# GpSimd's long subtractions in four pieces, v's halves made by ScalarE and VectorE, and v's largest turned one slot after its last product

## The chip, the core and the metric

The kernel runs on one core of a Trainium2 chip. The metric is the device time of one execution in microseconds, as the median of several executions. TensorE multiplies matrices, VectorE, ScalarE and GpSimd work on vectors, and SyncE issues DMAs. Each engine runs its own row of instructions in order; between engines there are only semaphores.

## What is computed

Three layers follow one another on the same activations, 4 batches of 576 positions:

```python
# 1: causal attention with decay, 8 heads of 64
scores = q @ k.T / 8 + cum[:, None] - cum[None, :]      # cum = cumsum(log f)
x = softmax(causal(scores)) @ v                         # heads side by side: 512 columns
# 2: low-rank mixing over positions, then a feed-forward part
u = x + (x.T @ U @ V).T                                 # U 576x32, V 32x576
y = u + relu(u @ w_ch1) @ w_ch2                         # 512 -> 2048 -> 512
# 3: four experts, each a causal attention of its own, the best two per position
q, k, v = y @ wq[e], y @ wk[e], y @ wv[e]
out += gate[e] * (softmax(causal(q @ k.T / 8)) @ v @ wo[e])
```

The result has float32 accuracy although the products run on narrower inputs: nearly every operand is held as two halves, a rounded one (name ending in `h`) and the rest that rounding left (ending in `l`), and a product is the sum of three matmuls, high by high, high by low and low by high.

## The kernel before

**Stages.** The first attention takes heads in pairs `p` = 0 to 15, four pairs a batch. For pair `p` the scores are multiplied and made into exponentials while the row maxima of pair `p+1` are found and the inputs of pair `p+2` loaded. The pairs of batch 0 run alone (the loop over `range(NP)`); in the pairs 4 to 15 (`later_batches`) matmuls of the feed-forward part of earlier batches are woven in by `fill`. Then the rest of the feed-forward part runs by itself (`fill_until`), and at the end the second attention with 16 heads `h`, four experts `e` for each batch `b`.

**What sets the order.** In `later_batches` and in the second attention the order on TensorE is the order of the code (`manual_schedule`). Everywhere else, and for all other engines throughout, a scheduler orders the instructions by times that it estimates while the program is built; an instruction that is made longer, shorter or moved to another engine can therefore change the order of others.

**The high and low halves.** `ffn_load` (L344) reads a block of 288 positions as `ust` [128, 4, 288], ScalarE rounds it to `uh` (L351), and GpSimd makes `ul` in one subtraction of 1152 columns (L352). In `ffn_hidden` (L359) eight matmuls take `uh`, and then four, one for each of the four slices of 288 columns, take `ul`. `load_y` does the same for the second attention with `yh` and `yl` (L770, L771). The weights' halves `w1l` and `w2l` (L341) are GpSimd subtractions too, of 512 columns, behind three VectorE operations on `wst` (L303, L305, L306).

**The values.** `value_scale` (L244) finds the largest |v|: VectorE reduces each partition to `am` (L247), TensorE turns that column into a row `amt` (L250), VectorE reduces the row to one number `ar`, whose exponent alone is kept (L252 to L254), TensorE spreads it over the partitions (`rsp`, L259), and VectorE's reciprocal gives `rs` (L261). `value_parts` (L264) multiplies `vr` by `rs` and 8192 on VectorE (L266), rounds it to float16 on ScalarE, `vh` (L267), and subtracts on GpSimd, `vl` (L268). `weighted_values` (L226) multiplies them with the two halves of the exponentials, `ph` and `pl` (L219, L220).

**The second attention's slots.** For each head the loop issues the first half of the scores (five matmuls), a slot, the second half (twelve), a slot, the products `ua` and `ub` for the row maxima of head `h+2` (L154, L162), a slot, the weighted values `av` of the head before, two slots, and the transposition `mt` of the row maxima (L178). A slot, `work_on(n)`, takes the next `n` pieces of the generators in `work`: projections `pq` of the next batch (`experts_qk`), its values `pv` and gates (`expert_values`), and the output products of the batch before (`expert_out`). A generator's `yield` ends a piece. The `ub` products need the score buffers (`ps2`, two of them), which ScalarE's exponentials `pf` (L218) empty.

Of the kernel before, what the change touches and what calls it, by code (L numbers as in the profile page):

```python
# [13 lines left out]
AF = mybir.ActivationFunctionType  # L14
OP = mybir.AluOpType
# [3 lines left out]
B, H, S, D = 4, 8, 576, 64  # L19
# [5 lines left out]
NT = 5  # L25
# [26 lines left out]
def f32(ap):  # L52
    return ap.bitcast(F32)
# [3 lines left out]
def kernel(  # L57
# [49 lines left out]


    ones1 = const.tile([1, P], BF16, name="ones1")
    nc.gpsimd.memset(ones1[:], 1.0)  # L110

    def make_heads(pl_, n, decay):

# [149 lines left out]

    def value_parts(vr, rs, vh, vl):  # L264

        nc.vector.tensor_scalar(vr, vr, rs[:, 0:1], VEXP, OP.mult, OP.mult)  # L266
        nc.scalar.copy(vh[:, :, :, 0:64], vr)  # L267
        nc.gpsimd.tensor_tensor(vl[:], vr, vh[:, :, :, 0:64], OP.subtract)  # L268

    def row_scales(av, rs, extra=None):  # L270

        den = small.tile([P, NT], F32, name="den")
        nc.vector.tensor_scalar(den[:], av[:, :, 64:65].rearrange("p t o -> p (t o)"),
                                1.0e-9 * PSCALE * VEXP, rs[:, 0:1], OP.add, OP.mult)
        rn = small.tile([P, NT], F32, name="rn")
        nc.vector.reciprocal(rn[:], den[:])
        if extra is not None:
            nc.vector.tensor_tensor(rn[:], rn[:], extra, OP.mult)
        return rn
# [64 lines left out]
    def ffn_load(b, c, first, fy):  # L344
        fu = cur["fu"]
        cs = slice(c * HC, c * HC + HC)
        ust = fy.tile([P, KT, HC], F32, name="ust", tag="yc")
        nc.sync.dma_start(ust[:], udram[b, :, :, cs])
        uh = fu.tile([P, KT, HC], F32R, name="uh")
        ul = fu.tile([P, KT, HC], F32R, name="ul")  # L350
        nc.scalar.copy(uh[:], ust[:])  # L351
        nc.gpsimd.tensor_tensor(ul[:], ust[:], f32(uh[:]), OP.subtract)  # L352
        if first:
            return uh, ul, ust
        yc = fy.tile([P, KT, HC], F32, name="yc", tag="yc")
        nc.sync.dma_start(yc[:], ydram[b, :, :, cs])
        return uh, ul, yc
# [109 lines left out]
    for i in range(2):  # L467
        vh_ = hpool.tile([P, 2, NT, 65], F16, name=f"vh{i}")
        vl_ = hpool.tile([P, 2, NT, 64], F16, name=f"vl{i}")
        nc.gpsimd.memset(vh_[:, :, :, 64:65], VEXP)  # L470
        vhs.append((vh_, vl_))
    NPAIR = B * NP
    st_in, st_rs, st_p = {}, {}, {}
# [287 lines left out]
    def load_y(b, yp, stp, tag):  # L761
        yh = yp.tile([P, KT, SP_], F32R, name="yh", tag="yh")
        yl = yp.tile([P, KT, SP_], F32R, name="yl")
        nc.gpsimd.memset(f32(yh[:, :, S:SP_]), 0.0)
        nc.gpsimd.memset(f32(yl[:, :, S:SP_]), 0.0)
        for c in range(NC):
            cs = slice(c * HC, c * HC + HC)
            st = stp.tile([P, KT, HC], F32, name="yst", tag=tag)
            nc.sync.dma_start(st[:], ydram[b, :, :, cs])
            nc.scalar.copy(yh[:, :, cs], st[:])  # L770
            nc.gpsimd.tensor_tensor(yl[:, :, cs], st[:], f32(yh[:, :, cs]), OP.subtract)  # L771
        return yh, yl

    y = load_y(0, sy0, fy, "yc")
# [80 lines left out]
    def expert_values(b, y):  # L855
# [4 lines left out]
        for t in range(NT):  # L860
# [6 lines left out]
                                     start=n == 0, stop=n == 3 * KT - 1)  # L867
                    n += 1
            nc.scalar.copy(vr[:, t, :], pv[:, 0:NV])
            yield  # L870
        vh = sy.tile([P, NT, E, 65], F16, name="vh3")
        vl = sy.tile([P, NT, E, 64], F16, name="vl3")
        nc.gpsimd.memset(vh[:, :, :, 64:65], VEXP)
        vv_ = vr[:, :, 0:E * D].rearrange("p t (e d) -> p t e d", e=E)
        rs = yield from value_scale(vv_)
        value_parts(vv_, rs, vh, vl)
# [90 lines left out]
    with tc.manual_schedule(engines={mybir.EngineType.PE}):  # L967
# [14 lines left out]
        for h in range(NH):  # L982
# [27 lines left out]
            work_on(2)  # L1010
            if m:
                one(m)
            if e == 3:
                work_on(2 if more else 1)
        expert_attend(B - 1, E - 1)
        work_on(100)
    for p_ in (ys[1], sy, att, hpool2, hpool, sy0, sw, small, psf, ps1, ps2, dram, const):
# [58 lines left out]
```

## Time and profile before

| | |
|---|---|
| median of 3 runs | 964.29 us (964.15 to 964.66) |
| profiled execution | 960.93 us |
| its span, first to last instruction | 959.2 us |
| mean granted TensorE clock | 0.944 |
| TensorE busy | 862.3 us (90%) |
| VectorE busy | 554.7 us (58%) |
| ScalarE busy | 416.5 us (43%) |
| GpSimd busy | 286.7 us (30%) |

In the rows below an engine's instruction stands with its line in the kernel, the tile that it writes and those that it reads. PE is TensorE, PEld its weight loads, DVE is VectorE, ACT is ScalarE and POOL is GpSimd. PEclk is the clock that TensorE was granted, 1.00 being full. A time in square brackets is how long the engine had nothing to do just before an instruction, followed by what ended that wait. An engine that is idle costs nothing unless TensorE, the busiest one, waits for it in the end.

### The profile page before, as it was taken

Reading aid. Unit: us, or ns where it says so; the run is one execution under the profiler, and the core shown is the slowest. Engines: PE = TensorE matmul, PEld = TensorE weight load, DVE = VectorE, ACT = ScalarE, POOL = GpSimd, SP = SyncE. Lnnn points to the kernel's source line nnn. Section 1 sums busy time; section 2 is a strip of 40 time slices with the busy share of each in tenths; the row PEclk is TensorE's granted clock in tenths of the full one; section 3 lists DMA queues with packets and bytes.
Section 4 is the critical chain, followed back from the end, with each engine's and each line's share of the span. In section 5 each row is a group of like instructions: output and inputs, shape, how many; then the busy total and the mean of one; then the engine's idle time right before and its main releaser. Section 6 shows DMA issues by size and latency. Waiting matters only on the chain.

```text
span 959.2 us, 19001 instructions
## 1 busy us (share of the span) xinstructions
PE 862.3 (90%) x7480; PEld 804.7 (84%) x7480; DVE 554.7 (58%) x1468; ACT 416.5 (43%) x784; POOL 286.7 (30%) x238
## 2 busy tenths in 40 slices
PE   4887778989999989989999999999999787999987
PEld 3766567888888878989999999999998787888965
DVE  7787677877666555542255652222225566667674
ACT  4556455655445544442134442222113444545454
POOL 8445354443433224021135333323023303001010
PEclk9987568999999999999999999999999787999999
DMA  6434454444533332103168653424006210212201
GB/s 172 136 84 133 146 155 140 120 133 130 138 108 84 104 109 60 52 14 112 50 222 286 217 203 111 149 73 127 28 26 183 65 40 12 75 38 65 49 36 66
DMA packets 68777, 101.94 MB, mean 106 GB/s; under 512 B 6608, under 2 KB 49424, under 8 KB 68688
## 3 DMA queue, kind: packets, MB, share of 16 engines
q1 hardware_dynamic: 64416, 92.47, 32.7%
q10 hardware_dynamic: 4272, 8.26, 2.3%
q8 instruction: 59, 0.97, 0.4%
q14 instruction: 30, 0.25, 0.1%
HBM read 60.33 MB, written 22.56 MB: 86 GB/s over the span
## 4 chain that ended last, share of the span: by engine, by line
PE 67%; DVE 12%; DMA 8%; ACT 6%; issue 4%; POOL 2%; SPq 1%; ACTq 0%; POOLq 0%; DVEq 0%
PE hps L366 19%; PE cps L381 18%; PE sc L209 8%; PE pq L823 4%; PE pv L866 3%; DMA ust<-udram 2%; DVE pl L220 2%; PE po L901 2%; PE av L236 2%; PE gp L548 2%; PE ub L162 2%; ACT pf L218 2%; DVE junk L173 2%; PE av L240 2%; PE av L238 2%
## 5 line engine op out<-in xcount | busy, mean ns | idle before, releaser
L381 PE MATMUL cps<-hh,w2h 128*128 128x288 f32 x512 | 156.3, 306 | 5.6 <-DVE yc L383 3.7
L381 PE MATMUL cps<-hh,w2l 128*128 128x288 f32 x512 | 153.1, 299 | 1.3 <-POOL w2l L341 1.3
L381 PE MATMUL cps<-hl,w2h 128*128 128x288 f32 x512 | 152.2, 297 | 0.0
L220 DVE TENSOR_TENSOR pl<-pf,ph 128x576 f16<-128x576 f32 x144 | 117.7, 823 | 51.8 <-ACT ph L219 51.2
L366 PE MATMUL hps<-uh,w1h 128*128 128x288 f32 x512 | 145.3, 305 | 0.2 <-ACT uh L351 0.2
L366 PE MATMUL hps<-uh,w1l 128*128 128x288 f32 x512 | 141.8, 299 | 0.0
L371 DVE SCALAR_TENSOR_TENSOR hl<-hps,hh 128x288 fp32r<-128x288 f32 x128 | 58.0, 453 | 119.1 <-ACT hh L370 119.0
L370 ACT ACTIVATE hh<-hps 128x288 fp32r<-128x288 f32 x128 | 52.3, 409 | 155.1 <-PE hps L366 154.9
L218 ACT ACTIVATE pf<-sc 128x576 f32<-128x576 f32 x144 | 84.0, 612 | 61.3 <-PE sc L209 55.9
L381 PEld LDWEIGHTS cps<-hh,w2h 128*128 128x128 f32 x512 | 97.9, 191 | 6.5 <-DVE yc L383 4.4
L381 PEld LDWEIGHTS cps<-hh,w2l 128*128 128x128 f32 x512 | 97.9, 191 | 1.5 <-POOL w2l L341 1.5
L366 PEld LDWEIGHTS hps<-uh,w1h 128*128 128x128 f32 x512 | 97.9, 191 | 0.6 <-ACT uh L351 0.4
L366 PEld LDWEIGHTS hps<-uh,w1l 128*128 128x128 f32 x512 | 97.9, 191 | 0.0
L381 PEld LDWEIGHTS cps<-hl,w2h 128*128 128x128 f32 x512 | 97.7, 191 | 0.0
L236 PE MATMUL av<-vh,ph 128*128 128x65 f16 x720 | 91.9, 206 | 1.9 <-DVE x L282 1.6
L366 PE MATMUL hps<-ul,w1h 128*128 128x288 f32 x512 | 89.4, 297 | 4.6 <-POOL ul L352 4.6
L238 PE MATMUL av<-vl,ph 128*128 128x64 f16 x720 | 90.5, 202 | 0.0
L240 PE MATMUL av<-vh,pl 128*128 128x65 f16 x720 | 90.0, 202 | 0.1
L209 PE MATMUL sc<-qa,ka 67*128 67x288 f32 (+4 forms) x288 | 83.0, 348 | 7.9 <-ACT pf L218 3.8
L219 ACT CAST ph<-pf 128x576 f16<-128x576 f32 x144 | 88.3, 638 | 1.6
L236 PEld LDWEIGHTS <-ph 128*128 128x128 f16 x720 | 70.9, 104 | 13.7 <-issue 5.6
L173 DVE CUSTOM_DVE_ANT_0 junk<-ub,maskm 128x448 bf16<-128x448 f32 x192 | 79.6, 414 | 3.2 <-PE ub L162 1.2
(160 smaller groups left out, 1966.1 us busy)
## 6 DMA issues: line engine op xcount, KB each, us to landing
raw<-in_w_dram SPq DMA_DIRECT2D x32, 512.0 KB
ust<-udram SPq DMA_DIRECT2D x22, 576.0 KB
qkt<-in_qk_dram SPq DMA_DIRECT2D x16, 576.0 KB
yc<-ydram SPq DMA_DIRECT2D x14, 576.0 KB
ydram<-yc SPq DMA_DIRECT2D x14, 576.0 KB
vr<-in_v_dram SPq DMA_DIRECT2D x16, 320.0 KB
udram<-ustage ACTq DMA_DIRECT2D x16, 288.0 KB
ydram<-ust SPq DMA_DIRECT2D x8, 576.0 KB
```

The costliest lines, as they stand in the source:

```text
L173: nc.vector.tensor_tensor_reduce(junk[0:n, 0:w], ub[0:n, bk, off:off + w], maskm[0:n, m0:m0 + w], 1.0, NEG, OP.add, OP.max, mx[0:n, t:t + 1])
L209: nc.tensor.matmul(ps[:, bk, off:off + w], wa, xa, start=bk not in banks[:n], stop=bk not in banks[n + 1:])
L218: nc.scalar.activation(pfv, view, AF.Exp, scale=ISC)
L219: nc.scalar.copy(ph[:, o0:o0 + n], pf[:, 0:n])
L220: nc.vector.tensor_tensor(pl[:, o0:o0 + n], pf[:, 0:n], ph[:, o0:o0 + n], OP.subtract)
L236: nc.tensor.matmul(av[0:m, it, :], ph[0:k, c:c + m], vh[0:k, jt, :], start=first, stop=False)
L238: nc.tensor.matmul(av[0:m, it, 0:64], ph[0:k, c:c + m], vl[0:k, jt, :], start=False, stop=False)
L240: nc.tensor.matmul(av[0:m, it, :], pl[0:k, c:c + m], vh[0:k, jt, :], start=False, stop=last)
L366: nc.tensor.matmul(ph[:], wa[:, k, fs], xa[:, k, :], start=n == 0, stop=n == 3 * KT - 1)
L370: nc.scalar.activation(hh[:], ph[:], AF.Relu)
L371: nc.vector.scalar_tensor_tensor(hl[:], ph[:], 0.0, f32(hh[:]), OP.max, OP.subtract)
L381: nc.tensor.matmul(pc[:], wa[:, t, dsl], xa[:], start=n == 0, stop=n == 3 * FT - 1)
```

## The change

The subtractions `ul` and `yl` are each issued as four, one for each slice of 288 columns. The scaling of `vr` is no longer an operation of its own: ScalarE scales while it rounds (`vh`), and VectorE scales and subtracts in one operation (`vl`). The factor 8192 moves into `ones1`, and so into `rs`; the column of `vh` that sums the exponentials holds 1 instead of 8192. In the second attention the last `pv` product and the reduction `am` are one piece, and the two extra slots after the fourth expert of a batch become one extra slot after each of the first two.

```diff
-    nc.gpsimd.memset(ones1[:], 1.0)
+    nc.gpsimd.memset(ones1[:], 1.0 / VEXP)
...
-        nc.vector.tensor_scalar(vr, vr, rs[:, 0:1], VEXP, OP.mult, OP.mult)
-        nc.scalar.copy(vh[:, :, :, 0:64], vr)
-        nc.gpsimd.tensor_tensor(vl[:], vr, vh[:, :, :, 0:64], OP.subtract)
+        nc.scalar.activation(vh[:, :, :, 0:64], vr, AF.Copy, scale=rs[:, 0:1])
+        nc.vector.scalar_tensor_tensor(vl[:], vr, rs[:, 0:1], vh[:, :, :, 0:64], OP.mult,
+                                       OP.subtract)
...
-                                1.0e-9 * PSCALE * VEXP, rs[:, 0:1], OP.add, OP.mult)
+                                1.0e-9 * PSCALE, rs[:, 0:1], OP.add, OP.mult)
...
-        nc.gpsimd.tensor_tensor(ul[:], ust[:], f32(uh[:]), OP.subtract)
+        for k in range(KT):
+            nc.gpsimd.tensor_tensor(ul[:, k], ust[:, k], f32(uh[:, k]), OP.subtract)
...
-            nc.gpsimd.tensor_tensor(yl[:, :, cs], st[:], f32(yh[:, :, cs]), OP.subtract)
+            for k in range(KT):
+                nc.gpsimd.tensor_tensor(yl[:, k, cs], st[:, k], f32(yh[:, k, cs]), OP.subtract)
...
             nc.scalar.copy(vr[:, t, :], pv[:, 0:NV])
-            yield
+            if t < NT - 1:
+                yield
...
-            if e == 3:
-                work_on(2 if more else 1)
+            if b == B - 1:
+                work_on(e == 3)
+            elif e < 2:
+                work_on(1)
```

The two `memset` lines of the `vh` column write 1.0 for `VEXP`. In the changed kernel the lines stand one to three further down from L352 on.

GpSimd's row in the feed-forward stage, before (`ul` of the blocks to come, `w1l` and `w2l` of the next quarter of the weights):

```order
L352 TENSOR_TENSOR ul<-ust,uh 128x1152 x3
L341 TENSOR_TENSOR w1l<-wst,w1h 128x4x128 x2
L352 TENSOR_TENSOR ul<-ust,uh 128x1152
L341 TENSOR_TENSOR w1l<-wst,w1h 128x4x128 x2
L352 TENSOR_TENSOR ul<-ust,uh 128x1152
L341 TENSOR_TENSOR w2l<-wst,w2h 128x512
L352 TENSOR_TENSOR ul<-ust,uh 128x1152
```

The same place in GpSimd's row of the changed kernel:

```order
L353 TENSOR_TENSOR ul<-ust,uh 128x288 x12
L341 TENSOR_TENSOR w1l<-wst,w1h 128x4x128 x2
L353 TENSOR_TENSOR ul<-ust,uh 128x288 x4
L341 TENSOR_TENSOR w1l<-wst,w1h 128x4x128 x2
L353 TENSOR_TENSOR ul<-ust,uh 128x288 x4
L341 TENSOR_TENSOR w2l<-wst,w2h 128x512
L353 TENSOR_TENSOR ul<-ust,uh 128x288 x4
```

Each long subtraction has become four; they keep their places among the weights' subtractions.

TensorE's row in the second attention, where batch 1's values end and the first head of batch 1 begins, before (`pv` values, `sc` scores, `amt` and `rsp` the two turns for v's largest):

```order
L866 MATMUL pv<-wah,yl 128x260
L178 MATMUL mt<-ident,mx_96 5x128
L250 MATMUL amt<-ident,am 1x128
L209 MATMUL sc<-qa_9049,ka_9051 128x288
...
L209 MATMUL sc<-maskt,identb 128x128
L259 LDWEIGHTS ones_87
L259 MATMUL rsp<-ar,ones_87 128x1
L209 MATMUL sc<-qa_9049,ka_9051 128x320
```

The same place in TensorE's row of the changed kernel:

```order
L868 MATMUL pv<-wah,yl 128x260
L178 MATMUL mt<-ident,mx_96 5x128
L209 MATMUL sc<-qa_9105,ka_9107 128x288
...
L209 MATMUL sc<-maskt,identb 128x128
L250 MATMUL amt<-ident,am 1x128
L209 MATMUL sc<-qa_9105,ka_9107 128x320
...
L259 LDWEIGHTS ones_87
L259 MATMUL rsp<-ar,ones_87 128x1
L154 MATMUL ua<-ka_8074,qa_8072 128x288 x2
```

`amt` has moved behind the first half of the scores, `rsp` behind the second half, and `ua` follows at once.

VectorE's row in the second attention, batch 3, before (`junk,mx` a piece of the row maxima, `gsm` and `gex` the gates):

```order
L261 RECIPROCAL rs<-rsp 128x1
L173 ISA junk,mx_98<-ub,maskm 128x192
L173 ISA mx_98 128x1
L806 TENSOR_REDUCE gsm<-gex 128x5
L266 TENSOR_SCALAR vr_11365<-vr_11365,rs 128x5x256
L173 ISA junk,mx_98<-ub,maskm 64x64
```

The same place in VectorE's row of the changed kernel:

```order
L261 RECIPROCAL rs<-rsp 128x1
L165 ISA junk,mx_98<-ua,maskm 128x576
...
L173 ISA junk,mx_98<-ub,maskm 128x448
L173 ISA mx_98 128x1
L809 TENSOR_SCALAR gsm<-gsm 128x5
L267 SCALAR_TENSOR_TENSOR vl_11560<-vr_11401,rs,vh_11559 128x1280
L173 ISA junk,mx_98<-ub,maskm 128x320
L173 ISA mx_98 128x1
```

Where the scaling stood before the last piece of the row maxima, `vl` now stands before the last three.

## Rows read from the trace of the kernel before

**Rows 1.** Stages: us; PE, PEld, DVE, ACT, POOL busy (instructions); PEclk, DMA share, GB/s.

```profile
0.00:128.00 128.00, 92.30 (x746) 79.01 (x747) 96.52 (x259) 70.72 (x125) 65.47 (x76) 0.83 0.47 139
128.00:430.00 302.00, 276.75 (x2680) 254.29 (x2680) 195.83 (x538) 151.79 (x281) 104.85 (x75) 0.95 0.35 101
430.00:722.00 292.00, 287.59 (x2164) 286.22 (x2161) 110.12 (x225) 79.00 (x148) 88.07 (x69) 0.99 0.41 132
722.00:959.20 237.20, 205.64 (x1901) 185.15 (x1899) 152.27 (x446) 114.98 (x230) 28.27 (x21) 0.93 0.24 64
```

**Rows 2.** TensorE's timeline: start us, duration us, instruction, idle before it.

```profile
138.29 1.01 PE L162 MATMUL ub<-ka,qa 66*128 66x448 f32 x2 [3.55 <-ACT pf L218]
...
249.29 0.79 PE L366 MATMUL hps<-ul,w1h 128*128 128x288 f32 x4 [1.86 <-POOL ul L352]
...
513.62 0.61 PE L381 MATMUL cps<-hh,w2h 128*128 128x288 f32 x1 [2.10 <-DVE yc L383]
...
538.97 0.40 PE L381 MATMUL cps<-hh,w2h 128*128 128x288 f32 x1 [1.25 <-DVE yc L383]
...
803.97 0.37 PE L250 MATMUL amt<-ident,am 128*1 128x128 f32 x1 [3.86 <-DVE am L247]
...
807.44 0.16 PE L259 MATMUL rsp<-ar,ones 1*128 1x1 bf16 x1 [1.93 <-DVE ar L254]
```

**Rows 3.** Short stretches behind four of these stalls, columns as in the first group.

```profile
139.00:144.00 5.00, 5.00 (x46) 4.85 (x45) 3.13 (x11) 1.20 (x4) 0.09 (x1) 0.50 0.57 185
...
514.00:517.00 3.00, 3.00 (x14) 3.00 (x14) 1.08 (x4) 0.93 (x2) 1.28 (x1) 0.50 0.55 183
539.00:542.00 3.00, 3.00 (x23) 3.00 (x23) 1.77 (x5) 0.62 (x1) 1.29 (x1) 1.00 0.62 200
...
804.00:813.00 9.00, 7.07 (x31) 6.66 (x32) 7.15 (x19) 4.80 (x8) 4.90 (x2) 0.50 0.01 3
```

**Rows 4.** VectorE's timeline, operations with two inputs in SBUF.

```profile
133.29 3.19 DVE L220 TENSOR_TENSOR pl<-pf,ph 128x576 f16<-128x576 f32 x1
...
247.79 2.06 DVE L220 TENSOR_TENSOR pl<-pf,ph 128x576 f16<-128x576 f32 x1 [1.59 <-ACT ph L219]
...
501.34 0.69 DVE L305 SCALAR_TENSOR_TENSOR wst<-raw,wst 128x512 int32<-128x512 int32 x1 [0.42 <-ACT raw L304]
...
510.73 2.46 DVE L305 SCALAR_TENSOR_TENSOR wst<-raw,wst 128x512 int32<-128x512 int32 x1 [0.80 <-ACT raw L304]
...
535.85 2.70 DVE L305 SCALAR_TENSOR_TENSOR wst<-raw,wst 128x512 int32<-128x512 int32 x1 [1.53 <-ACT raw L304]
...
803.84 2.61 DVE L791 TENSOR_TENSOR gt<-vr 128x80 f32<-128x80 f32 x1
```

**Rows 5.** GpSimd's timeline at 249 and 510 us.

```profile
249.20 1.88 POOL L268 TENSOR_TENSOR vl<-vr,vh 128x640 f16<-128x640 f32 x1
...
509.99 2.65 POOL L352 TENSOR_TENSOR ul<-ust,uh 128x1152 fp32r<-128x1152 f32 x1 [0.52 <-PE cps L381]
```

**Rows 6.** Groups by line and shape, GpSimd: count, busy us, mean ns, idle before.

```profile
L748 POOL TENSOR_TENSOR wal<-st,wah 128x512 fp32r<-128x512 f32 x4 | 5.2, 1293 | 22.1 <-ACT wah L747 22.1
...
L748 POOL TENSOR_TENSOR wal<-st,wah 128x260 fp32r<-128x260 f32 x4 | 3.0, 749 | 11.9 <-ACT wah L747 11.9
```

**Rows 7.** The same view, the scaling and the rounding of v.

```profile
L266 DVE TENSOR_SCALAR vr<-vr,rs 128x640 f32<-128x640 f32 x16 | 14.4, 898 | 0.1
...
L266 DVE TENSOR_SCALAR vr<-vr,rs 128x1280 f32<-128x1280 f32 x4 | 4.0, 1008 | 0.1
...
L267 ACT CAST vh<-vr 128x640 f16<-128x640 f32 x16 | 11.7, 729 | 11.2 <-DVE vr L266 11.2
...
L267 ACT CAST vh<-vr 128x1280 f16<-128x1280 f32 x4 | 5.1, 1264 | 7.6 <-DVE vr L266 7.6
```

**Rows 8.** The chain that ended last, at 807 us: start us, us, what.

```profile
807.60 2.67 PE sc L209 x12
```

**Rows 9.** The page's group of ScalarE's exponentials.

```profile
L218 ACT ACTIVATE pf<-sc 128x576 f32<-128x576 f32 x144 | 84.0, 612 | 61.3 <-PE sc L209 55.9
```

More of the change, by code (lines that the diff above doesn't have):

```diff
@@ L469 @@
         vl_ = hpool.tile([P, 2, NT, 64], F16, name=f"vl{i}")
-        nc.gpsimd.memset(vh_[:, :, :, 64:65], VEXP)
+        nc.gpsimd.memset(vh_[:, :, :, 64:65], 1.0)
         vhs.append((vh_, vl_))
@@ L869, in expert_values @@
             nc.scalar.copy(vr[:, t, :], pv[:, 0:NV])
-            yield
+            if t < NT - 1:
+                yield
         vh = sy.tile([P, NT, E, 65], F16, name="vh3")
         vl = sy.tile([P, NT, E, 64], F16, name="vl3")
-        nc.gpsimd.memset(vh[:, :, :, 64:65], VEXP)
+        nc.gpsimd.memset(vh[:, :, :, 64:65], 1.0)
         vv_ = vr[:, :, 0:E * D].rearrange("p t (e d) -> p t e d", e=E)
```

## Prediction

> **What bounds the kernel now.** I read the page first, then the engines' busy time by stage, then TensorE's stalls in order of time, then the granted clock behind each stall, and last what VectorE and GpSimd did there. By stage [rows 1] this is four programs, with TensorE the busiest engine in all but the first: to 128 us the first attention alone (TensorE busy 92.3 of 128 us), to 430 us attention and feed-forward woven together (276.8 of 302), to 722 us feed-forward alone (287.6 of 292), then the second attention (205.6 of 237.2). The time to be had is TensorE's idle time, 36, 25, 4 and 32 us, and what follows it.
>
> What follows is the clock. TensorE's stalls of 3.55 us at 138 us and 2.10 us at 514 us [rows 2] stand ahead of stretches at 0.50, the lower of the two levels (1.2 against 2.4 GHz); behind the stall of 1.25 us at 539 us it stays at 1.00 [rows 3]. In the second attention 804 to 813 us is at 0.50, behind a stall of 3.86 us.
>
> Several of these stalls begin on VectorE while GpSimd works. A rearranging operation on `wst` takes 0.69 us when GpSimd is quiet, and 2.46 and 2.70 us beside a long `ul` subtraction. `pl` takes 3.19 us, where its 576 columns at the quiet rate make 0.78; `gt`, 80 columns, takes 2.61 us beside `yl` [rows 4]. The held one ends an ordinary duration after GpSimd's instruction does: `ul` from 509.99 ends at 512.64 [rows 5], the `wst` operation at 513.19. So a long GpSimd subtraction holds VectorE's two-input operations until its own end.
>
> The Trainium skill, page "SBUF — State Buffer", section "Who interferes with whom", says that a VectorE instruction with two SBUF inputs and a GpSimd instruction that reads SBUF exclude each other, the first to issue keeping the shared ports for its whole length. The holds above agree. The rule also speaks against this change, as the second rival below.
>
> **Part 1: `ul` and `yl` in four pieces.** On GpSimd 512 columns take 1.293 us and 260 take 0.749 [rows 6]; on the line through both, a piece of 288 takes 0.81 us. Four take 3.24 us where one takes 2.65, so a hold shrinks to at most 0.81 us, and the last quarter comes 0.6 us later.
>
> At 133 us: `pl` starts at 133.29 and ends at 136.48; held by one piece at most, it ends by 133.29 + 0.81 + 0.78 = 134.9. The `ub` stall of 3.55 us hangs on it through the `pf` buffer and ScalarE: −1.6 us. Between 0 (another wait there ends as late) and −1.6 − 2.5, the half of the 5 us at 0.50 from 139 us [rows 3].
>
> At 510 us: the first piece of `ul` ends at 510.80, so `wst` at 511.5 instead of 513.19, and the addition to `yc` behind it follows; the stall of 2.10 us becomes 0.4, below the 1.25 us that left the clock alone. −1.7, and −1.5 for half of the 3 us at 0.50: −3.2 us (between −1.0, if part of the hold stays, and −3.6).
>
> At 536 us: `wst` ends by 535.85 + 0.81 + 0.69 = 537.35 instead of 538.55: −1.2 us (0 to −1.25, the whole stall).
>
> Twice, at 249 us and in the same way at 359 us, TensorE waits for `ul` itself, 1.86 us [rows 2]. Each `ul` matmul now waits for its own piece, but the four stand together behind the `uh` ones and the last needs the last piece: 0.6 us later, less three of four matmuls already done (the four take 0.79 us). That is +0.2 at each. If VectorE's `pl` of 0.78 us gets a turn between two pieces, another 0.8 at one of them: +1.2 us together, between −1 and +2. The other loads come early enough that another step's hidden matmuls cover 0.6 us.
>
> **Part 2: v's halves.** Out go 20 scalings on VectorE (16 at a mean of 0.898 us, 4 at 1.008, holds included [rows 7]) and 20 subtractions on GpSimd. In come 20 VectorE subtractions with two SBUF inputs, at the quiet rate of `wst` 0.86 us for 640 columns and 1.7 for 1280; ScalarE's 20 conversions stay (0.729 and 1.264 us), now started by `rs` instead of by the scaling. VectorE's time stays the same sixteen times and grows by 0.7 us four times. If the new ones are held as well, by 0.81 us each, it is 16 us more. In the woven stage, where TensorE is 92% busy, matmuls cover them: 0; with that cover gone 12 times 0.81, 10 us. GpSimd's freed time counts for nothing by itself. The new part is a wait: `vl` stands in VectorE's row and waits for ScalarE's `vh`; queued behind it are row maxima and the division by the sums, which TensorE waits for. That is the third rival. The `memset` constants cost nothing: the same instructions with another value.
>
> **Part 3: the turns.** The largest of v (`am`) is now issued with the last v product, and its transposition `amt` comes behind the next head's first five score matmuls; the twelve others then stand ahead of `rsp`. Twelve took 2.67 us [rows 8], so five take 1.1. Batch 1, from 800 us: `amt` waits 3.86 us because ScalarE's last copy of v stands behind two `yh` copies, which the new order leaves there. The five go into that stall, and the twelve into the 1.93 us before `rsp` [rows 2]. But the `pq` products that stood between the scores and `ub` are gone from there, so `ub` waits for two exponentials of 0.612 us [rows 9]: −1.1 − 1.9 + 1.2 = −1.8. Batch 0, from 749 us: twelve scores that ran before `amt` run after it, while `am` ends at the same time: +2.7, of which I take four fifths to fall into the waits that now stand behind `amt` (`rsp`, then `ub`): +0.5. Batch 3, from 910 us: `vl` (1.7 us, after a `vh` of 1.26) stands before three of the row maxima that `mt` waits for; of these 2.9 us I take two thirds to lie beside the `av` products: +1.0. Batch 2 keeps its pattern: 0. Sum −0.3 us, between −4 (the stalls go, and the clock stretch behind one shortens) and +4 (nothing saved in batch 1, the two losses larger).
>
> **The first attention** is ordered by the scheduler on TensorE too, and the new operations have reshuffled it on every engine. I find no chain that is clearly longer or shorter: 0, between −3.6 and +3.6, a tenth of its 36 idle microseconds [rows 1].
>
> **Sum.** −1.6 − 3.2 − 1.2 + 1.2 − 0.3 = −5.1 us. The profiled execution took 960.93 us (span 959.2), so 955.8 after. The median of the runs shown is 964.29, 3.36 us above that execution: I predict 959.2 us.
>
> **Rivals.** 1. *The clock gives more back.* If the stalls at 138 and 804 us get short enough, 5 us at 0.50 behind the one and 9 us (TensorE busy for 7.07 of them [rows 3]) behind the other run at full rate: 2.5 + 3.5 us more, 953.2 us. For: the 1.25 us stall left the clock up. Against: by my own sums about 2 and 2.8 us of these two stalls remain.
>
> 2. *Taking turns.* Behind one long hold VectorE was free; now each of `gt`, `eq` and `pl` can meet a piece of its own, and each one let in makes GpSimd's last piece later. Then the place at 133 us gives 0.8, the waits for `ul` at 249 and 359 us cost 1.7 each, the second attention loses 1.5: −0.8 − 3.2 − 1.2 + 3.4 + 1.5 = −0.3, 964.0 us, no change that can be told. For: a `vl` on GpSimd, right behind a long `ul`, took 1.88 us [rows 5], and a held `pl` of 2.06 us, from 247.79 to 249.85 [rows 4], ended within it, so VectorE does get a turn between two GpSimd instructions. Against: at 510 and 536 us the operation that TensorE waits for comes right behind the first held one. The skill's rule, named above, asks for this rival: two holders, one after the other, whatever their length.
>
> 3. *VectorE waits for ScalarE (slower).* `vl` blocks VectorE's row until `vh` is there: 0.73 us in five pairs of the first attention, 0.7 + 1.26 us in four batches of the second, 3.7 + 7.8 = 11.5 us if all of it is exposed: −5.1 + 11.5, 970.7 us. It outweighs the gain once 5.1 of the 11.5 us lie on TensorE's path. For: in both stages many of TensorE's stalls end with a VectorE operation. Against: ScalarE no longer waits for the scaling, 11.2 + 7.6 us in all [rows 7], so `vh` comes sooner.
>
> **How the numbers follow.** Forecast 0.48 (its own range 956 to 962.3), rival 1 0.12, rival 2 0.20, rival 3 0.20. The range 952.5 to 967 leaves out the outer part of rival 1 and over half of rival 3. 0.2% is 1.9 us, about what a measurement of this kernel can tell from no change: faster than 962.4 holds the forecast, rival 1 and a little of rival 2, 0.61; the same 0.19; slower 0.20.
>
> **What would show it.** Right: no VectorE operation like `wst`, `pl` or `gt` over 1.7 us; no stall over 1 us near 510 and 536 us, and the clock at 1.00 there; `rsp` without a wait in batches 1 and 3. Rival 2: `ul`'s four pieces spread over more than 3.5 us with `pl` between them, and stalls on `ul` over 2.5 us. Rival 3: VectorE idle before `vl`, ended by `vh`, and longer stalls on row maxima. The prediction is wrong if the first attention alone ends more than 3.6 us sooner or later, or if the second attention moves by more than 4 us.

## The result, and the profile after

The changed kernel takes 967.45 us (median of 14 runs, 961.76 to 974.95) beside 962.20 us of the kernel before (14 runs, 956.75 to 965.29): ratio 1.0066, 95% interval 1.0038 to 1.0094. It is slower, by some 6 us (3.7 to 9.0 by the interval); 959.2 us was predicted, 5.1 us less than the 964.29 of the three runs that were known then. The ratios here and below leave out one run of e13 (3034 us) and the profiled run of e16 (979.26 us), which stand far above the other runs of the same kernels. Its profiled execution took 971.99 us, 11.1 us more than that of before, at a span of 970.2 us and a mean granted clock of 0.947.

The stages of the kernel after, with the same bounds and columns as in [rows 1]:

```profile
0.00:128.00 128.00, 92.46 (x691) 79.04 (x692) 90.60 (x240) 67.56 (x118) 54.52 (x68) 0.93 0.43 126
128.00:430.00 302.00, 277.32 (x2632) 253.55 (x2631) 197.21 (x550) 152.81 (x280) 96.73 (x80) 0.94 0.36 106
430.00:722.00 292.00, 288.10 (x2205) 284.63 (x2205) 106.62 (x227) 82.60 (x156) 92.07 (x112) 0.99 0.40 133
722.00:970.20 248.20, 218.75 (x1958) 197.10 (x1956) 153.57 (x451) 115.75 (x231) 27.25 (x49) 0.91 0.22 61
```

In the first 128 us of this execution TensorE did 55 matmuls fewer than before (691 instead of 746), although its clock was higher (0.93 against 0.83); in a second execution of the same kernel (e4) it was 743, so one execution does not say where the kernel fell behind. Stages by the clock on the wall mix up what is late with what is slow, so the table below goes by landmarks in TensorE's timeline: the first mixing product (`gp<-x`, a group of them for each pair of heads), the sixth, the last feed-forward product (`cps`), the transposition `amt` of batch 3's values in the second attention, and the last matmul. Each column counts from the landmark before it, in us. Times are those of the one profiled execution of each kernel; the ratios are of all timed runs.

| kernel | to 1st `gp` | to 6th `gp` | to last `cps` | to batch 3's `amt` | to the end | ratio to before (95%) |
|---|---|---|---|---|---|---|
| before | 47.6 | 129.0 | 545.9 | 189.8 | 42.8 | 1 |
| copy of before (e5) | 47.7 | 129.3 | 545.5 | 190.1 | 42.8 | 0.9994 (0.9973 to 1.0016) |
| after | 51.0 | 132.5 | 546.7 | 186.8 | 49.1 | 1.0066 (1.0038 to 1.0094) |
| after, again (e4) | 51.1 | 129.3 | 544.7 | 187.0 | 49.2 | 1.0101 (1.0061 to 1.0141) |
| pieces (e1) | 48.5 | 136.6 | 550.2 | 189.8 | 49.2 | 1.0113 (1.0069 to 1.0157) |
| `ul` only (e6) | 47.2 | 132.7 | 554.6 | 190.1 | 49.6 | 1.0135 (1.0090 to 1.0180) |
| `yl` only (e7) | 47.7 | 130.5 | 545.5 | 187.1 | 44.2 | 1.0003 (0.9985 to 1.0021) |
| `ul` from 430 us, `yl` (e11) | 48.6 | 131.9 | 546.0 | 192.1 | 44.6 | 0.9991 (0.9962 to 1.0020) |
| halves (e2) | 51.2 | 133.7 | 546.6 | 192.3 | 44.9 | 1.0108 (1.0068 to 1.0148) |
| halves, batch 0 only (e17) | 51.5 | 131.4 | 547.4 | 189.9 | 42.8 | 1.0108 (1.0079 to 1.0136) |
| halves, woven only (e18) | 48.8 | 135.0 | 542.1 | 192.9 | 44.7 | 1.0019 (0.9992 to 1.0046) |
| halves, second only (e12) | 47.6 | 131.7 | 545.3 | 189.4 | 42.0 | 1.0012 (0.9981 to 1.0042) |
| turns (e3) | 47.0 | 132.4 | 549.9 | 190.6 | 49.5 | 1.0073 (1.0041 to 1.0105) |
| turns, not batch 3 (e14) | 48.2 | 131.1 | 544.3 | 187.3 | 48.5 | 1.0014 (0.9981 to 1.0047) |
| pieces and turns (e8) | 46.9 | 128.0 | 549.2 | 187.7 | 48.8 | 1.0105 (1.0071 to 1.0140) |
| after, first attention kept (e13) | 47.8 | 128.5 | 543.4 | 186.6 | 49.4 | 1.0004 (0.9978 to 1.0029) |
| e13 without batch 3's turn (e15) | 47.6 | 133.6 | 545.2 | 186.7 | 48.5 | 0.9982 (0.9952 to 1.0013) |
| before + 7 matmuls (e9) | 46.8 | 129.0 | 546.8 | 192.2 | 48.4 | 1.0105 (1.0075 to 1.0135) |
| before + 14 matmuls (e10) | 47.1 | 127.8 | 546.1 | 193.8 | 42.8 | 1.0076 (1.0048 to 1.0104) |
| after + 14 matmuls (e16) | 51.5 | 135.8 | 546.8 | 190.1 | 49.2 | 1.0075 (1.0044 to 1.0106) |

One execution's second and third column move by some 5 us with the clock that it happened to get (the second holds the first attention's long half-clock stretches). The first and the last repeat within 0.1 us for the same kernel (before and its copy, after and e4); yet among eight kernels that are the same up to 700 us, but for GpSimd's `yl` (before, e3, e5, e7, e9, e10, e12, e14), the first is 46.8 to 48.2. Where the new turns reach batch 3 (after, e3, e4, e8, e13, e16), `amt` stands twelve score matmuls earlier in TensorE's row, so some 1.6 us of work have moved from the fourth column to the fifth.

Much of what was predicted of the single stalls came. TensorE's timeline of the kernel after (start, duration, instruction, idle before it), the rows that answer to [rows 2] first, and then three that were not foreseen:

```profile
142.74 0.63 PE L162 MATMUL ub<-ka,qa 66*128 66x448 f32 x4
...
256.40 0.40 PE L367 MATMUL hps<-ul,w1h 128*128 128x288 f32 x1 [0.86 <-POOL ul L353]
...
508.58 0.40 PE L382 MATMUL cps<-hh,w2h 128*128 128x288 f32 x1 [0.18 <-DVE yc L384]
...
807.58 0.37 PE L250 MATMUL amt<-ident,am 128*1 128x128 f32 x1 [3.31 <-DVE am L247]
...
811.69 0.16 PE L259 MATMUL rsp<-ar,ones 1*128 1x1 bf16 x1 [1.37 <-DVE ar L254]
...
16.34 0.38 PE L178 MATMUL mt<-ident,mx 128*5 128x128 f32 x1 [2.57 <-DVE mx L173]
...
32.74 1.22 PE L209 MATMUL sc<-qa,ka 67*128 67x320 f32 x3 [2.63 <-ACT pf L218]
...
162.55 0.61 PE L382 MATMUL cps<-hh,w2h 128*128 128x288 f32 x1 [4.30 <-ACT w2h L340]
```

The stall on `ul` is 0.86 us at the longest of its four pieces instead of 1.86, that of 2.10 us on `yc` is 0.18. The stall of 3.55 us on `ub` is gone too, but the runs do not show it to be the pieces' work: the copy of before had 1.77 us there, the pieces without the halves (e1, e6, e8) 1.54 to 2.37, and the halves without the pieces (e2) none. Two signs of the prediction did not come: `rsp` still waits 1.37 us in batch 1, and outside the feed-forward `pl` still takes up to 2.50 us (at 41 us). The clock, by stretches of the kernel after (columns of [rows 1]): full from 442 to 750 us, the whole feed-forward alone, and half, 1.2 GHz, behind the late `w2h` and in the last batch:

```profile
442.00:750.00 308.00, 304.55 (x2276) 301.68 (x2276) 117.71 (x260) 87.79 (x168) 102.20 (x132) 1.00 0.43 139
920.00:936.00 16.00, 14.66 (x95) 12.21 (x95) 10.94 (x36) 6.79 (x14) 0.00 (x0) 0.50 0.01 2
163.00:172.00 9.00, 7.46 (x65) 6.83 (x65) 6.19 (x20) 2.87 (x5) 2.83 (x3) 0.50 0.62 187
```

By group (counts, busy us, mean ns; they answer to [rows 7], and to `ul` in [rows 5]) the means of the new operations are above the prediction's 0.81, 0.86 and 0.73 us:

```profile
L353 POOL TENSOR_TENSOR ul<-ust,uh 128x288 fp32r<-128x288 f32 x88 | 71.5, 845 | 73.3 <-ACT uh L351 69.3 <-PE hps L367 3.7
...
L267 DVE SCALAR_TENSOR_TENSOR vl<-vr,rs,vh 128x640 f16<-128x640 f32 x16 | 19.1, 1192 | 1.1 <-ACT vh L266 1.1
...
L266 ACT ACTIVATE vh<-vr,rs 128x640 f16<-128x640 f32 x16 | 13.3, 832 | 8.6 <-DVE rs L261 8.6
```

But the means hold what VectorE and GpSimd take from each other. A piece of `ul` that meets none of VectorE's two-input operations takes 0.79 to 0.82 us, and nine of the sixteen `vl` take 0.87 to 0.89; the others end 0.68 us behind a GpSimd subtraction and take 1.15 to 1.89. Only `vh` costs more by itself, by 0.10 us.

### The profile page after: what moved, and what is told of

Read it like the earlier page. It is cut to its first block, busy times and chain, and to the rows that moved or that the text cites. A ratio compares the mean times of both kernels' runs of the same rounds, so it can differ in the third digit from the quotient of the medians.

```text
span 970.2 us, 19065 instructions
## 1 busy us (share of the span) xinstructions
PE 876.6 (90%) x7480; PEld 814.3 (84%) x7480; DVE 548.0 (56%) x1468; ACT 418.7 (43%) x784; POOL 270.6 (28%) x308
## 5 line engine op out<-in xcount | busy, mean ns | idle before, releaser
L220 DVE TENSOR_TENSOR pl<-pf,ph 128x576 f16<-128x576 f32 x144 | 114.6, 800 | 32.6 <-ACT ph L219 32.0
L236 PE MATMUL av<-vh,ph 128*128 128x65 f16 x720 | 94.1, 208 | 2.5 <-DVE x L282 1.6
L367 PE MATMUL hps<-ul,w1h 128*128 128x288 f32 x512 | 91.8, 298 | 4.2 <-POOL ul L353 4.1
L238 PE MATMUL av<-vl,ph 128*128 128x64 f16 x720 | 92.6, 204 | 0.4 <-DVE vl L267 0.4
L240 PE MATMUL av<-vh,pl 128*128 128x65 f16 x720 | 92.1, 204 | 0.1
L353 POOL TENSOR_TENSOR ul<-ust,uh 128x288 fp32r<-128x288 f32 x88 | 71.5, 845 | 73.3 <-ACT uh L351 69.3
```

Source lines behind the costliest of these rows:

```text
L220: nc.vector.tensor_tensor(pl[:, o0:o0 + n], pf[:, 0:n], ph[:, o0:o0 + n], OP.subtract)
L236: nc.tensor.matmul(av[0:m, it, :], ph[0:k, c:c + m], vh[0:k, jt, :], start=first, stop=False)
L238: nc.tensor.matmul(av[0:m, it, 0:64], ph[0:k, c:c + m], vl[0:k, jt, :], start=False, stop=False)
L240: nc.tensor.matmul(av[0:m, it, :], pl[0:k, c:c + m], vh[0:k, jt, :], start=False, stop=last)
L353: nc.gpsimd.tensor_tensor(ul[:, k], ust[:, k], f32(uh[:, k]), OP.subtract)
L367: nc.tensor.matmul(ph[:], wa[:, k, fs], xa[:, k, :], start=n == 0, stop=n == 3 * KT - 1)
```

## The experiments

Each expectation names its own theories. From e6 on, A is that small moves of the program redraw where TensorE's clock is halved, and that this decides; B that the added instructions themselves cost; C, formed after the first runs, that the change of order in the first attention costs.

**The three parts alone, and all (e1 to e4).** e1 has the change's two hunks on `ul` and `yl`, e2 those on `ones1`, `value_parts`, `den` and the two `memset`, e3 the `yield` and the slots, e4 all.

> Only ul and yl in four pieces; the first attention keeps its old order. Theory (the pieces help, the loss comes from the other two parts): 2 to 5 us faster than before, no TensorE stall over 1 us between 500 and 540 us, clock at 1.00 there. Rival (pieces and VectorE take turns on the shared ports, so the pieces lose): within 2 us of before or slower, stalls on ul at 249 and 359 us over 2.5 us.

> Only v's halves made by ScalarE and VectorE; the order of the first attention on every engine becomes that of the changed kernel. Theory (the reordered first attention delays the first weights): 4 to 8 us slower than before, the first hidden product 4 to 6 us later than 127 us, a stall of over 3 us on w2h near 160 us. Rival (VectorE waits for vh): slower by about as much, but lost in the second attention, with VectorE idle before vl. Second rival (this part costs nothing): within 2 us.

> Only the turns and slots of the second attention. Theory of the prediction: 0 to 2 us faster, the second attention about as long as before (232.6 us from the last feed-forward product to the last matmul). Rival (the emptied slots of the fourth expert leave TensorE idle before the row maxima and its clock falls in the last batch): 3 to 6 us slower, the second attention 236 us or more, a stretch of over 10 us at half clock near 920 us.

> The whole change once more, a second profile beside the three parts. If the parts add up, its time is the sum of the three differences within 3 us. If the long stretch at half clock in the last batch belongs to the new order it is here again; if it was chance of that one execution, the last batch takes as long as in the kernel before.

Each part alone lost 7 to 11 us, and all together no more. So the parts do not add; and as e3 gives TensorE, ScalarE, VectorE and GpSimd the instructions of before in the same order until 747 us, its profiled 7 us of delay up to there can't be its edit: that is one launch's clock.

**A control (e5).** The kernel before, unchanged.

> A copy of the kernel before, word for word, as a control. If the losses of 7 to 10 us of the three single parts are real, the copy comes out at 1.000, within 0.002. If they are spread of the clock from launch to launch, the copy shows such ratios too, up to 1.007. Its profile is the second look at the end of the kernel before: if the 3.4 us at half clock in batch 3 of the second attention are a property of the kernel, they return (under 7.5 us); if the first profile was a lucky one, the stretch is 7 to 17 us, as in the variants, and the last 43 us (behind the last transposition of the largest of v) become 45 to 49.

0.9994, and the last batch 42.8 us again: the method tells 0.2%, and the short half-clock stretch at the end belongs to the kernel before.

**Which pieces (e6, e7).** e6 has the `ul` hunk alone, e7 the `yl` hunk.

> Only the subtraction for the weights in four pieces, the one of y whole. Theory A (the clock falls for longer because small times have moved; the moved stalls themselves are worth what the prediction said): the feed-forward alone 2 to 3 us shorter than before, the total anywhere from -3 to +9 us, the rest of the difference being time at half clock. Theory B (the pieces themselves cost, as more turns on shared ports): the feed-forward gains nothing and TensorE's stalls grow by more than 3 us in sum, the total +7 to +9 us.

> Only the subtraction for y in four pieces, which touches nothing ahead of 722 us. Theory A (clock): up to 722 us the program is that of the kernel before, so its time there differs only by the spread of the clock, within 3 us; the second attention gains 2 to 3 us between the first two transpositions of batch 0 and 1 and may lose up to 7 at half clock in batch 3: total -3 to +6 us. Theory B (pieces cost): +3 us or more, with longer stalls in the second attention.

`yl` costs nothing in sum. `ul` costs 13 us, and 8 of them stand at one place, between the seventh and the eighth mixing product (32.8 us; 25.1 before). ScalarE's conversions of `w2` in the kernel before, and below them those of e6 and TensorE's waits there (timelines):

```profile
209.21 0.62 ACT L340 CAST w2h<-wst 128x512 fp32r<-128x512 f32 x1 [0.31 <-DVE ar L253]
216.25 0.62 ACT L340 CAST w2h<-wst 128x512 fp32r<-128x512 f32 x1
```

```profile
210.45 0.62 ACT L340 CAST w2h<-wst 128x512 fp32r<-128x512 f32 x1
219.39 0.62 ACT L340 CAST w2h<-wst 128x512 fp32r<-128x512 f32 x1
228.48 0.62 ACT L340 CAST w2h<-wst 128x512 fp32r<-128x512 f32 x1
```

```profile
229.15 0.61 PE L382 MATMUL cps<-hh,w2h 128*128 128x288 f32 x1 [2.61 <-ACT w2h L340]
232.74 0.61 PE L382 MATMUL cps<-hh,w2l 128*128 128x288 f32 x1 [2.98 <-POOL w2l L341]
```

With `ul` in pieces the scheduler sets the conversions behind other work: the last one stands 12 us later, and the feed-forward catches up with it. The pieces themselves are innocent: TensorE's waits for `ul` there are 0.35, 0.86 and 0.36 us around 260 us, 1.57 in sum, where before had one of 1.86.

**No halves (e8).** The hunks of e1 and e3 together.

> The change without the value halves: four pieces and the new turns, the first attention in the order of the kernel before on every engine. Theory C (the halves cost 4 to 6 us in the first attention, by the new order and by the weights that come late at 158 us): 962 us beside 968 of the whole change, 0 to +2 us against before. Theory A (clock alone): as slow as the whole change, +6 to +8 us, with the stalls of before in the first attention and more time at half clock.

1.0105: Theory C's 962 us failed as stated, because the late `w2` of e6 is here too (2.61 and 3.04 us of stall, ahead of matmuls at 222 and 225 us), and the 8 us with it (33.1 us between the seventh and the eighth mixing product). In the whole change they aren't: with the halves the order there is another, the last conversion comes in time, and that stretch takes 24.5 to 25.0 us (after, e4, e16). So the parts do not add.

**A shift (e9, e10).** Seven, then fourteen needless matmuls before the second attention's first; TensorE's order is otherwise that of before.

```diff
+            for _ in range(7 if not delayed else 0):
+                nc.tensor.matmul(pq[:], wah[:, 0, w0:w0 + P], yh[:, 0, cs], start=True, stop=True)
```

> The kernel before with 7 needless matmuls of 288 columns (0.294 us each at full clock, 2.06 us) at the head of the second attention; TensorE's order is otherwise that of before. Theory A (how long TensorE stays at half clock behind a stall depends on where in time the stall falls, so any shift redraws it, and the kernel before stands at a lucky place): the time moves by something else than 2.1 us, between 0 and +9, with the stalls of before but other half-clock stretches, above all in the last batch (3.4 us before). Rival (the loss is made by the edits themselves): +2.1 us within 1.5, last 43 us unchanged.

> The same with 14 needless matmuls, 4.1 us. Theory A: not twice the effect of the 7, but 0 to +11 us, by the half-clock stretches that happen to come. Rival: +4.1 us within 1.5, last 43 us unchanged.

They cost 10 and 7 us (1.0105, 1.0076), but they are not the mere shifts that were meant. TensorE's timeline of e9, the seven, the next matmul, and a wait behind them:

```profile
722.40 1.09 PE L822 MATMUL pq<-yh,wah 128*128 128x288 f32 x7
723.33 0.29 PE L826 MATMUL pq<-yh,wah 128*128 128x288 f32 x1
...
734.37 0.37 PE L826 MATMUL pq<-yh,wah 128*128 128x288 f32 x1 [2.91 <-DVE kb L852]
```

The seven take 0.93 us and the fourteen of e10 1.87, not 2.06 and 4.1: a matmul of 0.29 us starts 0.13 us behind the one before it. And the scheduler has set VectorE's and ScalarE's rows anew: TensorE waits 2.91 us for `kb` (3.12 in e10) where before waited 0.80, and batch 0's `amt` comes 3.8 us later in both. So the two runs do not part Theory A from its rival.

One place parts them. At batch 3 the two kernels have the same stalls at nearly the same time. First e9, TensorE's timeline, then stretches of it (columns of [rows 1]):

```profile
916.65 0.74 PE L162 MATMUL ub<-ka,qa 66*128 66x448 f32 x4 [1.29 <-ACT pf L218]
...
919.01 0.16 PE L259 MATMUL rsp<-ar,ones 1*128 1x1 bf16 x1 [1.62 <-DVE ar L254]
```

```profile
917.00:918.00 1.00, 0.39 (x4) 0.33 (x3) 1.00 (x4) 0.24 (x1) 0.00 (x0) 0.78 0.00 0
...
922.00:934.00 12.00, 12.00 (x69) 9.92 (x69) 8.71 (x20) 5.45 (x12) 2.52 (x1) 0.50 0.01 2
```

And e10:

```profile
916.57 0.74 PE L162 MATMUL ub<-ka,qa 66*128 66x448 f32 x4 [1.29 <-ACT pf L218]
...
918.93 0.16 PE L259 MATMUL rsp<-ar,ones 1*128 1x1 bf16 x1 [1.62 <-DVE ar L254]
```

```profile
917.00:918.00 1.00, 0.31 (x4) 0.26 (x3) 1.00 (x4) 0.17 (x1) 0.00 (x0) 1.00 0.00 0
918.00:919.00 1.00, 0.07 (x1) 0.00 (x0) 1.00 (x6) 0.00 (x0) 0.00 (x0) 0.86 0.00 0
...
922.00:934.00 12.00, 11.25 (x100) 8.92 (x100) 9.80 (x26) 6.09 (x14) 2.54 (x1) 0.99 0.07 25
```

The same two waits, 1.29 and 1.62 us, and the clock halved 1.4 us before `rsp` in e9 (0.78 over the stretch from 917: 0.44 us of it at half) and 0.2 us before it in e10. In e10 it is full again behind 922; in e9 it stays at half until 934.6, although TensorE is busy throughout 922 to 934, and in those 12 us it gets through 69 matmuls instead of 100. Theory A holds for this place: the length of the stall does not decide what it costs. Twelve of the profiled executions have these two stalls (1.28 or 1.29 and 1.62 or 1.63 us). Where the clock fell 0.1 to 0.2 us before `rsp`, it was back after 3.4 us (before, e5, e10, e17); where it fell 0.4 to 1.5 us before, after 17.1 us (e1, e6, e9, e14, e15); where 1.5 to 1.8 us before, after 6.8 us (e2, e11, e18). The last column of the table goes with it: 42.8, 48.4 to 49.6, 44.6 to 44.9 us. That sorts twelve executions; no run tests it.

**Pieces without the woven stage (e11).** `ul` in pieces only for loads behind 430 us, `yl` as in the change.

```diff
-        nc.gpsimd.tensor_tensor(ul[:], ust[:], f32(uh[:]), OP.subtract)
+        if cur.get("alone"):
+            for k in range(KT):
+                nc.gpsimd.tensor_tensor(ul[:, k], ust[:, k], f32(uh[:, k]), OP.subtract)
+        else:
+            nc.gpsimd.tensor_tensor(ul[:], ust[:], f32(uh[:]), OP.subtract)
```

> The four pieces for the loads from 430 us on (feed-forward alone) and for y, the loads in the woven stage whole. If the 8 us that the pieces alone lose around 225 us come from the order in which the scheduler then sets the weight conversions there (a w2 conversion 12 us later, two stalls of 2.6 and 3.0 us and 10 us at half clock), that loss is gone: until 432 us as before within 3 us, feed-forward alone 287.5 us (290.0 before), a1 to a2 50 us (52.9 before); the last batch is a draw of the clock: total -5 to +2 us. If the pieces themselves cost, +5 us or more.

0.9991: the 11 us of e1 are gone, so they came with the woven stage's pieces (e1's last batch, at 49.2 us, was long as well).

**Halves by place (e12, e17, e18).** `value_parts` gets a flag; without it the three instructions are those of before, with 1.0 for `VEXP`.

```diff
-        value_parts(vr[:], st_rs[p], *vhs[p % 2])
+        value_parts(vr[:], st_rs[p], *vhs[p % 2], p < NP)
```

e17 has `p < NP`, e18 `p >= NP`, e12 sets the flag in the second attention alone.

> The value halves only in the second attention (the first attention keeps the scaling on VectorE, the rounding on ScalarE, the difference on GpSimd). If the halves lose in the first attention, by its new order (3.5 us in the first 50 us, and the late w2 conversion at 160 us, 2.5 us of stall and the clock behind it): 0 to +2 us against before, where the halves everywhere gave +10. If they lose by VectorE's row waiting for ScalarE in the second attention (rival 3 of the prediction): +4 us or more, with longer stalls on row maxima or on the largest of v behind 750 us.

> The value halves only in the first batch of the first attention (four pairs of heads, the first 130 us), the one part of it where the scheduler orders TensorE too. If the halves lose there, by VectorE's row waiting for ScalarE's vh (1.1 us before the first vl) and by the new order: 50.5 to 51.5 us to the first mixing product (47.6 before), +5 to +10 us in all, ratio 1.005 to 1.011, as the halves everywhere. If they lose in the woven stage: ratio 1.000 within 0.002.

> The value halves only in batches 1 to 3 of the first attention (the woven stage), TensorE's order as before throughout. If matmuls cover the longer VectorE operations there, as the prediction put it: ratio 1.000 within 0.003. If the late w2 conversion at 160 us (4.3 us of stall beside 1.8) comes from the halves of these batches: that stall is there and the ratio 1.003 to 1.008.

1.0012, 1.0108 and 1.0019: four of the twenty uses, those of batch 0, make the whole loss of the halves, some 10 us. TensorE's waits in e17, which answer to the last three rows of after above:

```profile
16.35 0.38 PE L178 MATMUL mt<-ident,mx 128*5 128x128 f32 x1 [2.16 <-DVE mx L173]
...
33.18 1.22 PE L209 MATMUL sc<-qa,ka 67*128 67x320 f32 x3 [2.63 <-ACT pf L218]
...
51.46 2.66 PE L553 MATMUL gp<-x,ut 128*96 128x128 f32 x10 [2.68 <-DVE x L287]
...
162.19 0.61 PE L386 MATMUL cps<-hh,w2h 128*128 128x288 f32 x1 [4.67 <-ACT w2h L345]
```

e18 came to the first `gp` at 48.8 us and never waited for `w2` by as much as 0.9 us. In the woven stage the prediction (matmuls cover the longer VectorE work) fits, within the interval's 0.5%.

**The change with the first attention kept (e13), and more (e14 to e16).** e13: halves in the second attention only, `ul` as in e11, `yl` and turns as in the change. e14: the turns, but with `if t < NT - 1 or b == B - 1` for the `yield` and the old slots for the last two batches. e15: e13 with e14's turns. e16: the whole change with e10's matmuls.

> The change with the first attention and the woven stage left as before: halves only in the second attention, ul's pieces only from 430 us on, y's pieces and the new turns as in the change. If two thirds of the loss sit in the new order of the first 200 us: 960 to 965 us, 3 to 7 us faster than the whole change in the same runs' terms, ratio to before 0.998 to 1.004, with the last batch (49 us beside 42.8) as the rest of the loss. If the loss is spread over everything, it stays at +6 us.

> The new turns in batches 0 to 2, and the values of batch 3 in the turns of before. If the turns lose by what they do to the last batch (2.6 us from a3 to a4, 6.7 us behind a4): a3 to a4 51.5 and a4 to the end 43 us again, the gains of 1 us each up to a1 and a2 remain, ratio 0.997 to 1.001, beside 1.0073 of the turns in all batches. If the clock alone decides: the last batch's half-clock stretch is a draw by the new shift (3.4 to 17 us), ratio 1.000 to 1.008.

> All that helped and nothing that lost: halves in the second attention, ul's pieces from 430 us on, y's pieces, the new turns except for the values of batch 3. By the gains seen in stages: 1 to 2 us in the feed-forward, 1 before a1, 1 to 3 between a1 and a2; less a draw of the clock in the last batch: 956 to 963 us, ratio 0.994 to 1.001.

> The whole change with the 14 needless matmuls (4.1 us) at the head of the second attention. If the place in time decides the half-clock stretch of the last batch, it may be shorter than the 16.5 us of the change and win back part of the 4.1 us: total -3 to +4 us against the whole change, a4 to the end 43 to 49 us. If the change's last batch is slow by its own order: +4.1 us, a4 to the end 49 us.

e13: 1.0004 beside 1.0066 and 1.0101 of the change. It leaves out two things at once, the halves in the first attention and `ul`'s pieces in the woven stage; no run leaves out the halves of batch 0 alone. That the pieces add nothing to the loss of the whole change is read from the traces (24.5 to 25.0 us at the place of e6's 8 us). e16 came out between the two measurements of the change, and its last batch stayed at 49.2 us: with the new order of batch 3 the last batch was long at every place in time that was tried (48.8 to 49.5 us in after, e3, e4, e8, e13, e16), so there it is not shown to be a draw; with the old order it was over 48 us in five of fourteen executions. e14 brought batch 3's order back and its last batch stayed long (48.5 us), against its expectation; its ratio, 1.0014, is yet below that of the turns in all batches, 1.0073. Why, is open. e15 has the lowest median of all, 960.65 us beside 961.47, but its interval takes in 1.

## Why the prediction was wrong

**The step that failed** is the one on the first attention: "I find no chain that is clearly longer or shorter: 0, between −3.6 and +3.6". The new order that the scheduler made of it, by the value halves of batch 0, costs some 10 us by itself (e17), and the cost falls behind the first attention, in the woven stage. The profiled executions, in us:

| kernels | to 4th `gp` | 5th to 6th `gp` | 7th to 8th `gp` |
|---|---|---|---|
| both stages as before (before, e3, e5, e7, e9, e10, e12, e14) | 110.4 to 116.1 | 29.8 to 31.8 | 25.0 to 26.5 |
| halves in batch 0 (after, e2, e4, e16, e17) | 111.2 to 116.7 | 34.3 to 37.6 | 24.5 to 26.0 |
| `ul` in pieces, no halves (e1, e6, e8) | 110.7 to 119.3 | 32.3 to 33.9 | 32.8 to 33.1 |

The five kernels with the halves in batch 0 come 3.4 to 3.9 us later to the first mixing product, the others at most 1.2. At the fourth, with 650 matmuls issued in every kernel, that is no longer seen. What lasts is some 5 us between the fifth and the sixth. There TensorE waits for the first quarter's `w2`, before and after:

```profile
156.94 0.40 PE L381 MATMUL cps<-hh,w2h 128*128 128x288 f32 x1 [1.84 <-ACT w2h L340]
```

```profile
162.55 0.61 PE L382 MATMUL cps<-hh,w2h 128*128 128x288 f32 x1 [4.30 <-ACT w2h L340]
```

In the five it waits 4.30 to 4.67 us, ahead of matmuls at 160 to 166 us, and the clock is at half behind it (0.50 from 163 to 172 us in after). ScalarE makes the third and fourth `w2h` at 149.0 and 156.3 us before, at 155.7 and 161.9 after: in the new order the weights' conversions stand later in its row. e18, with the halves only behind batch 0, has no such wait. The rest of e17's 10 us sits at no single place.

What delays the first mixing product is not the wait of the third rival. That wait can be seen in the profile of after; VectorE's timeline at 11 us, before and then after:

```profile
11.35 1.39 DVE L266 TENSOR_SCALAR vr<-vr,rs 128x640 f32<-128x640 f32 x1
12.66 0.74 DVE L165 CUSTOM_DVE_ANT_0 junk<-ua,maskm 128x576 bf16<-128x576 f32 x1
...
13.56 0.62 DVE L173 CUSTOM_DVE_ANT_0 junk<-ub,maskm 128x448 bf16<-128x448 f32 x1
```

```profile
11.56 0.74 DVE L165 CUSTOM_DVE_ANT_0 junk<-ua,maskm 128x576 bf16<-128x576 f32 x1
...
13.40 1.15 DVE L267 SCALAR_TENSOR_TENSOR vl<-vr,rs,vh 128x640 f16<-128x640 f32 x1 [1.10 <-ACT vh L266]
14.47 0.61 DVE L173 CUSTOM_DVE_ANT_0 junk<-ub,maskm 128x448 bf16<-128x448 f32 x1
```

But in e4, e16 and e17 `vl` starts without any wait and ends no sooner. VectorE's row of e17, and GpSimd's at the same time:

```profile
12.53 2.03 DVE L268 SCALAR_TENSOR_TENSOR vl<-vr,rs,vh 128x640 f16<-128x640 f32 x1
```

```profile
12.48 1.39 POOL L522 TENSOR_TENSOR qb<-qkt,qb 64x576 fp32r<-64x576 f32 x1
```

In all five `vl` ends at 14.54 to 14.56 us, 0.68 us behind the end of that `qb`, whenever it began: it is held, as `wst` was by `ul`. The prediction had named this hold ("If the new ones are held as well, by 0.81 us each"), but priced it for the woven stage alone. Four row maxima that TensorE waits for stand behind it: `mt` comes at 16.34 instead of 15.44. The rest of the 3.4 us is order. ScalarE now makes the next pair's `qa` and `ka` among the `ph`, and TensorE's wait for `pf` at 30 us is 2.62 or 2.63 us in the five (0.92 in before, but up to 2.19 in others of its order). At the first mixing product itself TensorE waits 1.53 to 2.83 us for `x`, under 0.6 in all others. The prediction had read the order of the later stages row by row and had taken the first 130 us, where 36 of TensorE's idle microseconds lie, as a draw.

**`ul` and `yl`.** Right in mechanism for the feed-forward: no `wst` over 1.2 us where the stalls of 510 and 536 us had been, no stall, full clock, and so in every kernel with the pieces there. In size, the feed-forward alone (from the last mixing product on) gave 2.2 to 2.6 us (290.0 to 287.4 and 287.8) instead of 4.4. The −1.6 us at 133 us rested on a stall that was half as long in the copy of before, and no run shows the pieces to shorten it. The waits for `ul` itself were priced at +1.2 us (the +0.2 at each does not follow from its own numbers: 0.6 us less three quarters of 0.79 is 0). They were not longer: 0.35, 0.86 and 0.36 us at 255 us instead of one of 1.86, and 0.32 to 0.91, 1.93 us in sum, at 365 instead of one of 2.28. Of the second rival (turns on the shared ports) the one sign came at five of 22 places, four pieces spread over more than 3.5 us (3.58 at 254 us, with a `pl` of 0.97 us among them; 3.10 undisturbed); the other, stalls on `ul` over 2.5 us, did not, and its cost neither. The Trainium skill, "SBUF — State Buffer", section "Who interferes with whom", had asked for it. What was not thought of: an edit to a GpSimd instruction moves ScalarE's and VectorE's rows too, through the scheduler (e6).

**Halves in the woven stage and the second attention:** 0, as predicted (e18, e12; within 0.5%).

**The turns** are the second step that failed. −0.3 us was the sum, between −4 and +4; alone they cost 7 us (e3, 1.0073). In the whole change the second attention went from 232.6 to 236 us: 3.0 us less up to batch 3's `amt` (189.8 to 186.8, `yl`'s pieces and the 1.6 us of moved work included) and 6.3 more behind it. There the new stalls are no longer than the old ones (1.26 on `amt`, 1.34 on `mt`; before 1.28 and 1.63), but half clock lasts for 17.1 us instead of 3.4. The first rival had asked whether the clock would give more back; it took. The prediction priced the clock only where a stall was to be shortened, and put down nothing for stalls that are merely moved.

So the account of the change is: some 5 us by the late `w2`, which the value halves of the first batch brought; −2.5 us in the feed-forward alone; and +3.4 in the second attention, where half clock in the last batch outweighs what the pieces and turns save. The last two nearly cancel (e13, 1.0004), and the first is about the result.

## What to carry to other kernels

Where a scheduler orders the rows, an edit's first cost is the order that it makes, and that cost can fall a stage behind the edit: read the new rows against the old ones, engine by engine, before pricing any stall. Test an edit to a shared helper by place: here sixteen of twenty uses were free and four cost 10 us. One profile can show a wait that decides nothing (the 1.10 us before `vl`); a second profile of the same kernel tells. And when stalls of the same length cost 3 us in one kernel and 17 in the next, don't credit or blame the edit for what the clock does; a control that adds a few matmuls may reorder the other engines too, so look at their rows before calling it a shift.

## What the runs showed of the hardware

Waits of 1.29 and 1.62 us were followed by half clock for 3.4 us (e10) or for 17.1 (e9), with the same work behind them; the clock fell 0.2 us before the second wait's end in the one and 1.5 in the other, and in e9 it stayed at half through 12 us in which TensorE was busy throughout. The same program's launches spread by 14 us (before, 957.1 to 971.4 over 29 runs), while in two profiled launches its stretches up to the first `gp` and behind batch 3's `amt` repeat within 0.1 us. A GpSimd subtraction of 288 columns took 0.79 to 0.82 us undisturbed (0.81 worked out from longer ones), four in a row 3.10, and one of 1152 columns 2.65. A VectorE subtraction with two inputs in SBUF and a scale, 640 columns, took 0.87 to 0.89 us (the rate of `wst` gave 0.86), and up to 2.03 when a GpSimd subtraction ran: it then ended 0.68 us behind it, in e17 as in after.
